# Attention and two expert layers on one core: freeing the queues after attention, and spreading the first batch's work over more slots

## The chip, the cores and the metric

One Trainium2 chip, one of its cores. The metric is the device time of one execution in microseconds (us); a kernel is run three times or more and the median is quoted. A profile comes from one further execution, so sums are made against that execution's own time.

## The reference

```python
def _attn_ref(q, k, v):            # q, k, v: (4, 8, 576, 64), float32
    scores = scale * np.matmul(q, k.transpose(0, 1, 3, 2))
    mask = block_i >= block_j      # blocks of 64 positions
    scores = np.where(mask, scores, -1000000000.0)
    attn = np.exp(scores - scores.max(-1, keepdims=True))
    attn = attn / (attn.sum(-1, keepdims=True) + 1e-09)
    return np.matmul(attn, v)
...
x = attn_out as (2304, 512)
h = x @ w_in                       # 512 -> 2048
g = np.maximum(h, 0.0) + alpha * np.minimum(h, 0.0)
x = g @ w_out                      # 2048 -> 512
h = x @ w2_in
g = np.where(h > 0.0, h, np.exp(np.minimum(h, 0.0)) - 1.0)
return g @ w2_out
```

The weights reach the kernel as 64-bit floats. Each is rebuilt on the chip as a float32 value.

## The kernel before

Every matrix product is made of three passes over a high and a low part of each operand (`PASSES`), so one product of 128x128 weights with 512 tokens over four chunks is twelve matmuls.

Attention runs over 16 pairs of heads, four pairs to a batch. `slot(k)` is one slot of its pipeline: the scores of one block of 128 queries, its maxima (VectorE), exponentials (ScalarE), the transposes of the block four slots back, and the products with the values that `products(k)` names. The first eight pairs (`n < WHOLE`) use `pv_whole`. Its first half has two chunks of keys. The second half has five, and all its matmuls stand in one slot, between that slot's scores and its transposes. Its `out()` then copies the sums from PSUM into `x1` (ScalarE for the high part, VectorE for the low part). The first 27 slots (`lead`) have attention alone. From there each slot of attention is followed by a piece of the first layer for a finished batch (`l1_beside`).

The first layer has 16 tiles of weights (`f`), the first eight in the pool `wA`. Units of 512, 512, 512, 512 and 256 tokens pass through it. After attention come stage A (units 3 and 4, tiles 0 to 7), stage B (all five units, tiles 8 to 15, in the pool `wB`) and stage C (all five units through the second layer, 16 tiles). One step of these stages is one `f`: `l1_h` (L499) or `l2_h` (L545) makes the hidden values, and two steps later `l1_y` (L587) or `l2_y` (L563) takes the gated values back. The gate of A and B is `neg` on ScalarE (L479), `g` on VectorE (L482), the high part on ScalarE (L486) and the low part on GpSimd (L81). The gate of C is `e` on ScalarE (L549), two operations on VectorE (L550, L551), the high part on ScalarE (L554) and the low part on VectorE (L81). Four PSUM banks hold the sums of a unit. At its end they are read out: in A by copies (`to_z`), in B by adding what A left (`z`, L594), whose halves go to memory for stage C. The next unit's sums start in the same banks.

`load_w` brings half a tile of weights and rebuilds it in pieces that it puts off by ticks (`later`, `end_tick`): `first` (ScalarE, L125 and L126), `bits` (VectorE, L130 to L132), `rounded` (GpSimd, L137), a copy (ScalarE, L145) and `last` (VectorE, L81). It has two buffers for the raw words and two for the rebuilt ones (`wraw`, `wword`). L125 needs a `wword` that `last` of the load two before has freed, and SyncE issues the next transfer into a raw buffer once L137 has read it. There are 16 such loads in and beside attention, then 48: 16 for tiles 8 to 15 of the first layer, 16 for tiles 0 to 7 of the second, and 16 for its tiles 8 to 15. The last 16 go into `wB`, whose tiles come free as the last unit of stage B is done with them.

The order of the work is written out by hand for all five queues: the program's order is each queue's order, and each queue runs its instructions one after the other. Where no such order is given, a planner in the compiler lays out each queue: at each point it takes, of the instructions whose inputs and buffers are there in its own model of time, the first in the program's order. The result is again one fixed order for each queue.

Of the kernel before, what the change touches and what calls it, by code (L numbers as in the profile page):

```python
# [11 lines left out]
U32 = mybir.dt.uint32  # L12
# [12 lines left out]
FH = NF // 2  # L25
# [16 lines left out]
def attention_moe_kernel(ctx: ExitStack, tc: tile.TileContext, qT, kT, v_a, v_b, w1, w2, alpha, out):  # L42
    nc = tc.nc
    pe, act, dve, pool_e = nc.tensor, nc.scalar, nc.vector, nc.gpsimd
# [24 lines left out]
    def take(name):  # L69
        r = rings[name]  # L70
        r.append(r.pop(0))
        return r[-1]
# [7 lines left out]
    def low_part(eng, out, x, high):  # L80
        return {"v": dve, "p": pool_e}[eng].tensor_tensor(out=out, in0=x, in1=f32(high), op=ALU.subtract)  # L81
# [13 lines left out]
    def later(ticks, emit):  # L95
        due.setdefault(tick[0] + ticks, []).append(emit)
# [13 lines left out]
    def load_w(layer, f, r):  # L110
        if r == 0:
            wt[layer, f] = w_pools[f // FH].tile([P, 2, 2 * DM], F32R, tag="w", name="w")
        t = wt[layer, f]
        raw = wraw_p.tile([P, 2 * DM], U32, tag="wraw", name="wraw")
        nc.sync.dma_start(out=raw, in_=(w1, w2)[layer][f, :, r * DM:(r + 1) * DM].bitcast(U32))
        pairs = raw.rearrange("p (n t) -> p n t", t=2)
        low, high = pairs[:, :, 0], pairs[:, :, 1]
        units = low.bitcast(I32)
        hi, lo = (t[:, k, r * DM:(r + 1) * DM] for k in range(2))
        word = []  # L120

        def first():
            w = wraw_p.tile([P, DM], F32, tag="wword", name="wword")
            word.append(w)
            act.activation(out=w, in_=high.bitcast(F32), func=AF.Abs)  # L125
            act.activation(out=units, in_=low, func=AF.Copy, scale=2.0 ** -29)  # L126

        def bits():
            w, wi = word[0], word[0].bitcast(U32)
            dve.tensor_scalar(w, w, F64_MIN, F64_MAX, ALU.max, ALU.min)  # L130
            dve.tensor_scalar(wi, wi, 3, 0x3FFFFFF8, ALU.logical_shift_left, ALU.bitwise_and)  # L131
            dve.scalar_tensor_tensor(  # L132
                out=wi, in0=high, scalar=0xC0000000, in1=wi, op0=ALU.bitwise_and, op1=ALU.bitwise_or)

        def rounded():
            w = word[0].bitcast(I32)
            pool_e.tensor_tensor(out=w, in0=w, in1=units, op=ALU.add)  # L137

        def last():
            low_part("v", lo, word[0], hi)  # L140
            ready.add((layer, f, r))
        later(2, first)
        later(3, bits)
        later(4, rounded)
        later(5, lambda: act.copy(hi, word[0]))  # L145
        later(6, last)

    def w_in(layer, f, part, kc):
        assert (layer, f, 0) in ready
# [15 lines left out]
    bank = [None] * 4 + [ps.tile([P, 512], F32, name=f"bank{i}") for i in range(4, 8)]  # L165
# [117 lines left out]
    def place(half, j):  # L283
        return (0, 128)[j] if half == 0 else 960 - 256 if j == 4 else 320 * j
# [47 lines left out]
    def x_tile(b):  # L332
        if b not in x1:
            x1[b] = xp.tile([P, 2, KC, 512], F32R, tag="x1", name="x1")
        return x1[b]

    def x_out(n, half, done):

        b, p = PAIRS[n]
        if half == 1:  # L340
            nc.sync.dma_start(out=xd[b][:, :, p, :], in_=f32(x1[b][:, :, p, :]))
            nc.sync.dma_start(out=xd[B][:, :, p, 64 * b:64 * b + 64], in_=f32(done))

    def parts_of_x(n, half):
        b, p = PAIRS[n]
        parts = [(slice(0, 256), lambda k: x_tile(b)[:, k, p, 256 * half:256 * half + 256])]
        tail = None
        if half == 1:
            tail = ap1.tile([P, 2, 64], F32R, tag="xtail", name="xtail")
            parts.append((slice(256, 320), lambda k: tail[:, k, :]))  # L350
        return parts, tail


    def pv_whole(n, half):
        s = st[n]
        q0, qn = HALF[half]
        nch = 2 if half == 0 else 5
        op = bank[take("o")]
        for j in range(nch):
            rows = 64 if j == 4 else P  # L360
            lo, o = max(0, P * j - q0), place(half, j)
            for x in range(2):
                pe.matmul(op[64 * x:64 * x + 64, lo:qn], s["v"][:rows, x, j, :],
                          s["pt", half, 0][:rows, x, o + lo:o + qn],
                          start=j == 0, stop=j == nch - 1, skip_group_check=True)

        def out():
            parts, tail = parts_of_x(n, half)
            for c, dst in parts:
                act.copy(dst(0), op[:, c])  # L370
                low_part("v", dst(1), op[:, c], dst(0))
            x_out(n, half, tail)
        return out
# [33 lines left out]
    LAG = 4  # L407
# [3 lines left out]
    def products(k):  # L411


        todo = []
        n, i = divmod(k - LAG - 4, 5)
        if i == 0 and 0 <= n < len(PAIRS):
            todo += [lambda: pv_whole(n, 0)] if n < WHOLE else [lambda: pv(n, 0, 0), lambda: pv(n, 0, 1)]
        m, i = divmod(k - LAG - 6, 5)
        if 0 <= m < len(PAIRS) and i < 2:
            if m >= WHOLE:  # L420
                todo.append(lambda: pv(m, 1, i))
            elif i == 0:
                todo.append(lambda: pv_whole(m, 1))
        return todo
# [37 lines left out]
        end_tick()  # L462

    X_DONE = [5 * (NPAIR * b + NPAIR - 1) + LAG + 6 + (NPAIR * (b + 1) > WHOLE) for b in range(B)]

# [133 lines left out]
    ET = mybir.EngineType  # L601
    with tc.manual_schedule(engines={ET.PE, ET.Activation, ET.DVE, ET.Pool, ET.SP}):
        ring("s", 0, 1)
        ring("t", 4, 5)
        ring("o", 6, 7)
        load_pair(0)
        split_k(0)
        split_q(0)

        todo_w = [(0, f, r) for r in range(2) for f in range(FH)]  # L610
        lead = X_DONE[0] + 2
        for k in range(lead):
            if k % 3 == 0 and k and len(todo_w) > FH:
                load_w(*todo_w.pop(0))
            slot(k)
        ring("t", 4, 5, 6)
        rings["o"] = rings["t"]
        ring("h", 7)


        k = lead
        for u in range(B - 1):
            parts = l1_beside(u)
            for j in range(20):
                if todo_w:
                    load_w(*todo_w.pop(0))
                next(parts)
                if k < LAST:
                    assert k <= X_DONE[u + 1] or j >= 18
                    slot(k)  # L630
                    k += 1
        assert k == LAST and not held

        att.close()
        ps = ctx.enter_context(pool("ps_all", 1, space=PSUM))
        bank[:] = [ps.tile([P, 512], F32, name=f"bank{i}") for i in range(8)]
        w_pools.append(ctx.enter_context(pool("wB", FH)))
        late_pools.append(ctx.enter_context(pool("late", 1)))  # L640
        ring("h", 6, 7, 0, 1)
        units = [("A", u) for u in range(B - 1, NU)] + [(k, u) for k in "BC" for u in range(NU)]
        fs = {"A": range(FH), "B": range(FH, NF), "C": range(NF)}
        steps = [(k, u, f) for k, u in units for f in fs[k]]
        first_of = {}
        for i, (k, u, f) in enumerate(steps):
            first_of.setdefault((k, u), i)
        lag = 2
        w_at = {}
        spread = [*range(8), *range(8, 16, 2), *range(16, 20)]  # L650
        for i in range(2 * FH):
            half = i // 2, i % 2
            w_at[spread[i]] = (0, FH + half[0], half[1])
            w_at[spread[-1] + 1 + i] = (1, *half)
            w_at[first_of["C", 0] - 2 + i] = (1, FH + half[0], half[1])
        gs = {}
        for i in range(len(steps) + lag):
            if i in w_at:
                load_w(*w_at[i])
            if i < len(steps):  # L660
                k, u, f = steps[i]
                if f == fs[k][1]:
                    n = units.index((k, u)) + 1
                    if n < len(units):
                        (load_x2 if units[n][0] == "C" else load_x1)(units[n][1])
                gs[i] = l2_h(u, f) if k == "C" else l1_gate(f, l1_h(u, f), UNITS[u])
            end_tick()
            if i >= lag:
                k, u, f = steps[i - lag]
                if k == "C":  # L670
                    l2_y(u, f, gs.pop(i - lag))
                else:
                    l1_y(k, u, f, gs.pop(i - lag))
            end_tick()
# [32 lines left out]
```

## Time and profile before

| | |
|---|---|
| median of three runs | 1105.73 us (1104.4 to 1106.81) |
| the profiled execution | 1103.71 us |
| its span, from the first to the last instruction | 1101.9 us |
| TensorE busy | 1002.6 us, 91% of the span |
| VectorE, ScalarE, GpSimd busy | 596.9, 463.7, 385.2 us |
| mean granted clock of TensorE | 0.968 |

TensorE is the engine with the most work. The profile cuts the span into stretches and gives each engine's busy time there, the clock that TensorE was granted (1.00 is 2.4 GHz, 0.50 is 1.2 GHz), and what each instruction waited for. 1.8 us of the execution lie outside the span.

### The profile page before, as it was taken

What the parts mean: (1) busy time and instruction counts of PE and PEld (TensorE: products, weight loads), DVE (VectorE), ACT (ScalarE), POOL (GpSimd) and SP (SyncE); (2) the same over time, 40 slices, a digit from 0 to 9 for tenths busy, and PEclk for the clock granted to TensorE, in tenths of its full rate; (3) what the DMA queues carried; (4) which work ended last, traced back from release to release, by engine and by line L of the source; (5) the groups of instructions that cost most, each with busy time, mean ns of one, the idle gap of its engine ahead of it and who ended that gap; (6) DMA issues with size and microseconds to landing.
All of it is one profiled execution on the core that took longest, in us unless ns stands there. A gap on an engine that the chain in (4) does not pass through costs nothing.

```text
span 1101.9 us, 14026 instructions
## 1 busy us (share of the span) xinstructions
PE 1002.6 (91%) x5072; PEld 805.8 (73%) x5072; DVE 596.9 (54%) x1067; ACT 463.7 (42%) x1017; POOL 385.2 (35%) x452
## 2 busy tenths in 40 slices
PE   6768769999999998997979998987899999999998
PEld 4446547778878887886758887865688888888887
DVE  5777875566666375657564325777433333333343
ACT  4666644575575344444443324444222222222222
POOL 5655664586686353545454332222000000000000
PEclk9898989999999998998989999998899999999999
DMA  4343322212211325536362345322200210110010
GB/s 143 102 156 97 127 89 87 83 57 94 85 54 52 136 98 192 166 123 225 120 224 99 115 154 181 105 77 76 95 20 1 77 39 1 39 39 1 1 39 20
DMA packets 50469, 101.58 MB, mean 92 GB/s; under 512 B 10592, under 2 KB 18784, under 8 KB 49760
## 3 DMA queue, kind: packets, MB, share of 16 engines
q1 hardware_dynamic: 50400, 100.69, 27.1%
q8 instruction: 40, 0.66, 0.3%
q14 instruction: 29, 0.24, 0.1%
HBM read 72.36 MB, written 28.31 MB: 91 GB/s over the span
## 4 chain that ended last, share of the span: by engine, by line
PE 54%; DVE 18%; ACT 9%; issue 5%; POOL 3%; DMA 3%; SPq 0%; ACTq 0%; POOLq 0%; DVEq 0%
PE bank L563 15%; PE bank L545 15%; PE bank L499 7%; PE bank L522 5%; PE bank L587 4%; DVE wword L132 4%; DVE w L81 4%; DMA wraw<-w 3%; PE bank L386 3%; ACT wword L125 2%; DVE g L482 2%; PE pair L234 2%; ACT wraw L126 2%; DVE wword L131 2%; PE bank L310 2%
## 5 line engine op out<-in xcount | busy, mean ns | idle before, releaser
L499 PE MATMUL bank<-x,w 128*128 128x512 f32 (+1 forms) x960 | 216.6, 376 | 10.7 <-ACT h L514 9.7
L545 PE MATMUL bank<-x,w 128*128 128x512 f32 (+1 forms) x960 | 215.1, 373 | 10.4 <-DVE w L81 7.5
L563 PE MATMUL bank<-w,gs 128*128 128x512 f32 x864 | 213.5, 394 | 8.7 <-DVE gs L81 5.6
L545 PEld LDWEIGHTS bank<-x,w 128*128 128x128 f32 x960 | 171.5, 191 | 43.7 <-DVE w L81 8.4
L499 PEld LDWEIGHTS bank<-x,w 128*128 128x128 f32 x960 | 169.7, 192 | 42.8 <-ACT h L514 11.8
L563 PEld LDWEIGHTS bank<-w,gs 128*128 128x128 f32 x864 | 162.3, 190 | 45.5 <-DVE gs L81 7.6
L587 PE MATMUL bank<-gs,w 128*128 128x512 f32 (+1 forms) x672 | 151.0, 372 | 23.0 <-DVE z L594 12.4
L587 PEld LDWEIGHTS bank<-gs,w 128*128 128x128 f32 x672 | 116.9, 195 | 49.5 <-issue 13.2
L81 POOL TENSOR_TENSOR gs<-g,gs 128x512 fp32r<-128x512 f32 (+1 forms) x80 | 96.1, 1201 | 155.6 <-ACT gs L486 155.4
L550 DVE TENSOR_SCALAR e<-e 128x512 f32<-128x512 f32 (+1 forms) x80 | 32.1, 401 | 188.5 <-ACT e L549 188.5
L137 POOL TENSOR_TENSOR wword<-wword,wraw 128x512 int32<-128x512 int32 x64 | 96.4, 1506 | 95.9 <-DVE wword L132 67.2
L549 ACT ACTIVATE e<-bank 128x512 f32<-128x512 f32 (+1 forms) x80 | 44.2, 553 | 171.6 <-PE bank L545 171.6
L88 POOL TENSOR_SCALAR p<-p,stat 128x128 f32<-128x128 f32 (+2 forms) x144 | 85.6, 612 | 61.7 <-DVE stat L275 43.2
L482 DVE SCALAR_TENSOR_TENSOR g<-neg,beta,bank 128x512 f32<-128x512 f32 (+1 forms) x56 | 37.5, 670 | 126.8 <-ACT neg L479 126.8
L125 ACT ACTIVATE wword<-wraw 128x512 f32<-128x512 f32 x64 | 43.0, 671 | 124.1 <-DVE w L81 96.6
L522 PE MATMUL bank<-gs,w 128*128 128x512 f32 x288 | 76.7, 409 | 10.2 <-ACT h L514 9.3
L554 ACT CAST gs<-e 128x512 fp32r<-128x512 f32 (+1 forms) x80 | 46.3, 579 | 82.7 <-DVE e L551 82.7
L264 ACT ACTIVATE p<-pair,stat 128x128 f32<-128x128 f32 (+3 forms) x128 | 67.0, 535 | 23.0 <-DVE stat L253 19.0
L132 DVE SCALAR_TENSOR_TENSOR wword<-wraw,wword 128x512 uint32<-128x512 uint32 x64 | 75.3, 1176 | 2.2
L81 DVE TENSOR_TENSOR gs<-e,gs 128x512 fp32r<-128x512 f32 (+1 forms) x80 | 51.0, 638 | 41.2 <-ACT gs L554 41.2
L81 DVE TENSOR_TENSOR w<-wword,w 128x512 fp32r<-128x512 f32 x64 | 66.5, 1039 | 7.2 <-ACT w L145 7.2
L522 PEld LDWEIGHTS bank<-gs,w 128*128 128x128 f32 x288 | 52.6, 193 | 20.9 <-ACT h L514 10.0
(84 smaller groups left out, 1170.8 us busy)
## 6 DMA issues: line engine op xcount, KB each, us to landing
wraw<-w SPq DMA_DIRECT2D x64, 512.0 KB, 3.5
xd<-x SPq DMA_DIRECT2D x16, 512.0 KB, 3.3
x<-xd SPq DMA_DIRECT2D x16, 512.0 KB, 8.3
yd<-ys SPq DMA_DIRECT2D x16, 512.0 KB, 5.7
x<-yd SPq DMA_DIRECT2D x4, 2048.0 KB, 8.2
qraw<-qT SPq DMA_DIRECT2D x16, 288.0 KB, 3.3
kraw<-kT SPq DMA_DIRECT2D x16, 288.0 KB, 3.6
vraw<-v_a SPq DMA_DIRECT2D x16, 256.0 KB, 4.0
```

The lines of the kernel that those rows point to most:

```text
L81: return {"v": dve, "p": pool_e}[eng].tensor_tensor(out=out, in0=x, in1=f32(high), op=ALU.subtract)
L88: return pool_e.tensor_scalar(out, x, 1.0 if scale is None else scale, 1.0, ALU.mult, ALU.mult)
L125: act.activation(out=w, in_=high.bitcast(F32), func=AF.Abs)
L132: dve.scalar_tensor_tensor(out=wi, in0=high, scalar=0xC0000000, in1=wi, op0=ALU.bitwise_and, op1=ALU.bitwise_or)
L137: pool_e.tensor_tensor(out=w, in0=w, in1=units, op=ALU.add)
L264: act.activation(out=p[:, x, :], in_=sb[:, x, :ext], func=AF.Exp, bias=stat[:, o + x:o + x + 1], accum_out=stat[:, 4 + o + x:5 + o + x])
L482: dve.scalar_tensor_tensor(out=g, in0=neg, scalar=beta[:, f:f + 1], in1=h, op0=ALU.mult, op1=ALU.add)
L499: pe.matmul(h, w_in(0, f, wp_, kc), x[:, xp_, kc, :n], start=kc == 0 and t == 0, stop=kc == KC - 1 and t == 2)
L522: pe.matmul(acc, w_out(0, f, wp_, m * P, P), gs[f][:, gp_, :n], start=f == 0 and t == 0, stop=f == FH - 1 and t == 2)
L545: pe.matmul(h, w_in(1, f, wp_, kc), x[:, xp_, kc, :], start=kc == 0 and t == 0, stop=kc == KC - 1 and t == 2)
L563: pe.matmul(acc, gs[:, gp_, tg * P:(tg + 1) * P], w_out(1, f, wp_, 0, DM), start=f == 0 and t == 0, stop=f == NF - 1 and t == 2)
L587: pe.matmul(acc, w_out(0, f, wp_, m * P, P), gs[:, gp_, :n], start=first and t == 0, stop=last and t == 2)
```

## The change

Three things are altered. The hand order for all five queues now ends with attention; from stage A to the end only TensorE keeps it, and ScalarE, VectorE, GpSimd and SyncE get the planner's order. The third operation of `bits` (L132) becomes a piece of its own, `sign`. For the eight loads of the lead (layer 0, `f < FH`, `r == 0`) `sign` and all pieces after it come one tick later; for all other loads `sign` stands right behind `bits`, as before. Last, in the first batch (pairs 0 to 3) the second half of `pv_whole` is cut in two: chunks 0 and 1 in one slot, chunks 2 to 4 and `out()` in the next.

```diff
             dve.tensor_scalar(wi, wi, 3, 0x3FFFFFF8, ALU.logical_shift_left, ALU.bitwise_and)
+
+        def sign():
+            wi = word[0].bitcast(U32)
             dve.scalar_tensor_tensor(
                 out=wi, in0=high, scalar=0xC0000000, in1=wi, op0=ALU.bitwise_and, op1=ALU.bitwise_or)
...
         later(3, bits)
-        later(4, rounded)
-        later(5, lambda: act.copy(hi, word[0]))
-        later(6, last)
+        slow = 1 if layer == 0 and f < FH and r == 0 else 0
+        later(3 + slow, sign)
+        later(4 + slow, rounded)
+        later(5 + slow, lambda: act.copy(hi, word[0]))
+        later(6 + slow, last)
...
-    def pv_whole(n, half):
+    def pv_whole(n, half, chunks=None):
...
-        op = bank[take("o")]
-        for j in range(nch):
+        chunks = chunks or range(nch)
+        if chunks[0] == 0:
+            s["op"] = bank[take("o")]
+        op = s["op"]
+        for j in chunks:
...
         def out():
+            if chunks[-1] < nch - 1:
+                return
...
             if m >= WHOLE:
                 todo.append(lambda: pv(m, 1, i))
+            elif 5 * m + LAG + 7 < LEAD:
+                todo.append(lambda: pv_whole(m, 1, (range(2), range(2, 5))[i]))
             elif i == 0:
                 todo.append(lambda: pv_whole(m, 1))
...
         assert k == LAST and not held
 
+
+    with tc.manual_schedule(engines={ET.PE}):
 
 
         att.close()
```

(`lead` also becomes `LEAD`, with the same value, 27.)

## Rows read from the trace of the kernel before

**Rows 1.** Windows: span start:end, length, busy us (x instructions) per engine, clock, DMA share.

```profile
0.00:88.59 88.59, 62.35 (x387) 39.80 (x387) 64.36 (x155) 50.48 (x144) 54.36 (x92) 0.92 0.38 125
...
375.40:671.00 295.60, 272.57 (x1321) 227.13 (x1321) 154.94 (x213) 124.45 (x230) 126.10 (x99) 0.97 0.46 155
671.00:784.56 113.56, 94.48 (x386) 73.95 (x385) 77.58 (x117) 46.12 (x83) 26.46 (x19) 0.92 0.29 97
784.56:1096.41 311.85, 311.84 (x1465) 261.61 (x1463) 111.99 (x203) 75.25 (x136) 0.00 (x0) 1.00 0.08 30
```

**Rows 2.** Chain that ended last, two of its pieces: start, length, engine and line.

```profile
577.18 2.72 PE bank L499 x12
...
661.08 1.44 PE bank L587 x12
```

**Rows 3.** Windows of five stretches between stage A and stage C, columns as before.

```profile
422.22:432.00 9.78, 4.73 (x26) 4.23 (x25) 8.07 (x14) 5.54 (x12) 4.64 (x4) 0.74 0.90 281
502.65:516.70 14.05, 8.24 (x26) 5.40 (x25) 10.53 (x14) 5.48 (x10) 5.55 (x5) 0.76 0.69 225
555.72:571.54 15.82, 8.19 (x25) 5.41 (x24) 12.04 (x16) 6.81 (x13) 5.57 (x5) 0.78 0.62 200
682.08:690.09 8.01, 4.88 (x14) 3.51 (x13) 5.71 (x12) 3.37 (x8) 2.03 (x3) 0.79 0.93 371
717.32:784.56 67.24, 51.28 (x193) 38.46 (x192) 45.13 (x66) 26.00 (x47) 13.74 (x9) 0.90 0.20 66
```

**Rows 4.** Timeline of TensorE at the end of a unit of stage B.

```profile
555.72 2.88 PE L499 MATMUL bank<-x,w 128*128 128x512 f32 x12
565.69 1.62 PE L587 MATMUL bank<-gs,w 128*128 128x512 f32 x3 [7.09 <-DVE z L594]
```

**Rows 5.** Timeline of VectorE there.

```profile
561.66 0.75 DVE L482 SCALAR_TENSOR_TENSOR g<-neg,beta,bank 128x512 f32<-128x512 f32 x1 [1.77 <-ACT neg L479]
...
564.87 0.68 DVE L594 TENSOR_TENSOR z<-bank,z 128x512 f32<-128x512 f32 x1
```

**Rows 6.** Timeline of ScalarE, once there and twice in stage C.

```profile
554.22 0.67 ACT L125 ACTIVATE wword<-wraw 128x512 f32<-128x512 f32 x1 [2.56 <-DVE w L81]
...
736.55 0.67 ACT L125 ACTIVATE wword<-wraw 128x512 f32<-128x512 f32 x1 [3.26 <-DVE w L81]
...
743.35 0.66 ACT L125 ACTIVATE wword<-wraw 128x512 f32<-128x512 f32 x1 [3.26 <-DVE w L81]
```

**Rows 7.** Groups by line from 671 to 784 us: count, busy, mean ns, idle before.

```profile
L81 DVE TENSOR_TENSOR w<-wword,w 128x512 fp32r<-128x512 f32 x15 | 25.8, 1717 | 0.0
L137 POOL TENSOR_TENSOR wword<-wword,wraw 128x512 int32<-128x512 int32 x16 | 24.2, 1510 | 69.9 <-DVE wword L132 66.6 <-ACT gs L554 3.3
L132 DVE SCALAR_TENSOR_TENSOR wword<-wraw,wword 128x512 uint32<-128x512 uint32 x16 | 11.5, 718 | 0.6
L551 DVE SCALAR_TENSOR_TENSOR e<-bank,e 128x512 f32<-128x512 f32 x16 | 11.1, 692 | 0.6
L81 DVE TENSOR_TENSOR gs<-e,gs 128x512 fp32r<-128x512 f32 x15 | 10.3, 684 | 0.0
...
L550 DVE TENSOR_SCALAR e<-e 128x512 f32<-128x512 f32 x16 | 6.9, 428 | 32.7 <-ACT e L549 32.7
L131 DVE TENSOR_SCALAR wword<-wword 128x512 uint32<-128x512 uint32 x16 | 6.8, 427 | 0.5
L130 DVE TENSOR_SCALAR wword<-wword 128x512 f32<-128x512 f32 x16 | 6.7, 418 | 0.0
```

**Rows 8.** DMA issues of the page: median us from issue to landing stands last.

```profile
wraw<-w SPq DMA_DIRECT2D x64, 512.0 KB, 3.5
```

**Rows 9.** Timeline of TensorE in the lead, at the second half of a pair's product.

```profile
64.96 0.35 PE L234 MATMUL pair<-kh,qh 64*128 64x128 f32 x2 [4.36 <-ACT p L264]
...
65.67 3.82 PE L363 MATMUL bank<-pt,vraw 128*64 128x320 f32 x20
```

**Rows 10.** Timeline of VectorE in the lead, around that product.

```profile
69.95 0.42 DVE L81 TENSOR_TENSOR x<-bank,x 128x256 fp32r<-128x256 f32 x1 [1.70 <-ACT x L370]
```

More of the change, by code (lines that the diff above doesn't have):

```diff
@@ L464, in attention_moe_kernel @@
     X_DONE = [5 * (NPAIR * b + NPAIR - 1) + LAG + 6 + (NPAIR * (b + 1) > WHOLE) for b in range(B)]
+    LEAD = X_DONE[0] + 2
     def load_x1(u):
@@ L610, in attention_moe_kernel @@
         todo_w = [(0, f, r) for r in range(2) for f in range(FH)]
-        lead = X_DONE[0] + 2
-        for k in range(lead):
+        for k in range(LEAD):
             if k % 3 == 0 and k and len(todo_w) > FH:
@@ L618, in attention_moe_kernel @@
         ring("h", 7)
-        k = lead
+        k = LEAD
         for u in range(B - 1):
```

## The prediction

> **What bounds the kernel now.** I read the windows first, cut where the stages meet. From 784.56 us to the last matmul TensorE is busy 311.84 of 311.85 us at full clock [rows 1]: that part cannot get shorter, since no matmul is removed. From 375.40 (the first matmul of stage A) to 784.56 it is busy 272.57 of 295.60 and 94.48 of 113.56 us, at a mean granted clock of 0.97 and 0.92 [rows 1]. So the second reading is what this stretch would take if TensorE never waited. The chain of waits shows twelve matmuls of 512 tokens taking 2.72 us and twelve of 256 tokens 1.44 us at full clock [rows 2]. By the loops there are 110 groups of the first kind in the stretch (16 in A's unit 3, 64 in B's units 0 to 3, and 16 `l2_h` and 14 `l2_y` of C's unit 0) and 32 of the second: 110 x 2.72 + 32 x 1.44 = 345.3 us. The stretch lasts 409.2. **63.9 us are lost there**: 42.1 with TensorE idle, and nearly all of the rest by matmuls at the low clock behind the idle times, as the clock columns of the five worst stretches show (0.74 to 0.90) [rows 3].
>
> These five hold 54.9 of it. At the ends of units: 9.78 us for two groups of 256 tokens (2.88), 14.05 and 15.82 us for two of 512 (5.44 each), 8.01 for one (2.72), so 6.9 + 8.6 + 10.4 + 5.3 = 31.2. In C's unit 0: 67.24 us for eight steps of 5.44, 43.5, so 23.7 [rows 3]. The other 9.0 are crumbs of one or two microseconds at other steps.
>
> Third, who is late. At the end of a B unit TensorE goes idle for 7.09 us until VectorE has added a sum out of its bank (`z`, L594) [rows 4]. The sum had been complete for longer than that. VectorE stood 1.77 us for `neg`, then ran `g` and the three decoding operations, and only then `z`, at 564.87 [rows 5]. `neg` in turn was late because ScalarE stood 2.6 us at L125 of the next load, whose `wword` the decoding had not freed, with `neg` behind it [rows 6]. In C it is the same ring: L125 waits 3.26 us for VectorE's `last`, `e` stands behind L125, VectorE's gate waits for `e`, and `last` stands behind the gate. One turn decodes one load and lets one step through, and takes 743.35 - 736.55 = 6.80 us, where TensorE needs 5.44 [rows 2, 6].
>
> So the loss is one of order in the queues, not of work: in the two windows VectorE is busy 154.94 and 77.58 us, 57% of the stretch, and ScalarE and GpSimd less [rows 1].
>
> **The change, part by part.** *The planner's order after attention* removes and adds no instruction. It moves four queues: `neg` or `e` no longer stands behind an L125 that has no buffer, `z` no longer behind decoding that came later than its sum, and on SyncE the loads of tokens and partial sums no longer behind a weight transfer that waits for a raw buffer. What can take the place of the ring is work, so I sum that. One load and one step of C cost VectorE 428 + 692 + 684 ns for the gate and 418 + 427 + 718 + 1717 for the decoding, 5.08 us [rows 7], under 5.44. The 1717 is a time with GpSimd's L137 beside it; the same shape in the gate takes 684 [rows 7]. GpSimd has 1.51 us. ScalarE has five operations on tiles no larger, so it has room. The last sixteen loads are the tight ones: `wB` comes free only as B's unit 4 ends, from about 656.8 (tile 10 is read back at 661.08, three groups of 1.44 after tile 8 [rows 2]); the weights of step 8 are wanted when that step begins, about 712 (717.32 less the 5.3 lost before it [rows 3]), and the sixteenth load when tile 15 is read back, 9 steps and a half of 5.44 later, about 764. Sixteen loads in 764 - 657 allow 6.7 us each, against 5.1 of VectorE. The first two can stand decoded up to the copy beforehand, since their buffers are no part of `wB`. So I take C's unit 0 as nearly unhindered.
>
> From both sides: the gain of this part is at most the 63.9, and the least, if the new order merely has other waits, is below nothing (second rival). What I leave standing: 1.1 us at each of the seven unit ends of the stretch, because four adds of about 0.7 us and the halves behind them still go through VectorE (7.7); 0.3 us at each of the sixteen short steps of 256 tokens, where the gate has half the time (4.8); and 3.4 for the rest, C's first steps and the start of A. That is 15.9, so 63.9 - 15.9 = **48 us gained**. The entries are my estimates; the ends are taken nearer to the crumbs than to the 8.6 and 10.4 of the ends with decoding beside them.
>
> Here a rule of the notes on the chip bears on the sum. The row shows `last` at 1717 ns beside L137 where its twin takes 684 [rows 7]. The Trainium skill (SBUF — State Buffer, "Who interferes with whom") says that GpSimd and VectorE share one pair of ports as an exclusive lock, so that the loser stands still for the other's whole instruction. The trace agrees: 1717 - 684 = 1.03 us, within L137's 1.51. By that rule a step with a load costs the pair 428 + 692 + 684 + 418 + 427 + 718 + 684 + 1510 = 5.56 us at most and not 5.08, 0.12 over TensorE's 5.44, and the sum would lose some 2 us more over sixteen loads.
>
> *The second product in two slots.* All its matmuls run 3.82 us at the low clock, in front of the slot's transposes and the next slot's scores [rows 9]. The first two chunks are 640 of its 1216 columns (320, 320, 320, 192, 64), 2.0 us; the other 1.8 go behind the next slot's scores, which come that much sooner. VectorE's wait of 1.70 us for the sums of it [rows 10] moves one slot on, to where maxima stand before it. This happens four times. Against it: the last `out()` now falls in slot 26, and its bank is the one that the first `l1_h` writes in slot 27; ScalarE's and VectorE's copies, about 1.2 us, then lie in TensorE's way once. *Decoding in smaller pieces* leaves VectorE's work as it is, but `bits` and the `last` of an earlier load (up to 2.25 us unhindered, by rows 7) no longer stand in one block before a slot's maxima. The lead is a ring of VectorE, ScalarE and TensorE: VectorE is busy 64.36 of 88.59 us [rows 1], and TensorE waits 4.36 us for exponentials once before such a product [rows 9]. The gain lies between -2 (the bank, and one more tick of decoding) and 24.2 (all of VectorE's idle time). Most of that idle time is the start and other waits, so I take **3 us**, nearer to the 1.70 of the one wait that is surely moved.
>
> The sum: 1103.71 - 48 - 3 = 1052.7 for the profiled execution, which lay 2.0 below the median of its runs. **Forecast: 1055 us.**
>
> **The rivals.**
> 1. *The planner packs the decoding.* It starts pieces of later loads as soon as an engine is free, at five loads to four steps, say. By the price of rows 7 a step then has 1.80 + 1.25 x 3.76 = 6.5 us of VectorE and GpSimd together, if they exclude each other, 1.06 over 5.44. Forty-eight loads take 38 steps: 40 us lost, less the slack of four groups (10.9 us) in each of two bursts, so 19 us of the gain: 1074. For it: GpSimd's and VectorE's times do stretch each other. Against: the gates come first in the program's order.
> 2. *The other side: the fixed order stands on transfers that come later than planned.* Weights land 3.5 us after issue in the median [rows 8]. If the plan reckons them 2 us earlier than the chip brings them, ScalarE stands at L125 with the gate behind it, at each load: 48 x 2 = 96 us, less 10.9 of slack once, 85 lost in place of 63.9: about 1124 with the lead's 3 us. It decides from about 1.6 us a load ((63.9 + 3 + 10.9) / 48). Against: the raw buffer is filled a load ahead, which hides most of a transfer.
> 3. *No change: the two buffers, not the order, set the pace.* Then a turn stays 6.8 us and the time within 1104 to 1107. Against: one load's own chain on VectorE and GpSimd is 0.42 + 0.43 + 0.72 + 1.72 + 1.51 = 4.8 us, some 7 with ScalarE's three, and two loads overlap.
> 4. *Better than forecast:* 6 us left standing, 10 gained in the lead: 1103.7 - 58 - 10 + 2 = 1038.
>
> **How the numbers follow.** Forecast 0.60, rival 1 0.18, rival 2 0.12, rival 3 0.04, rival 4 0.06. The forecast's own range is 1043 (9 left standing, 8 in the lead) to 1068 (24 left standing, -2 in the lead). The range of 8 in 10 takes in rivals 1 and 4 with their edges, 1036 to 1094, and leaves rivals 2 and 3 out. Faster by over 0.2% (about what a measurement of this kernel can tell from no change): 0.60 + 0.18 + 0.06 = 0.84; the same 0.04; slower 0.12.
>
> **What would show it.** Right: in the changed profile the idle times of TensorE before L587 released by `z` shrink to about a microsecond, those before L545 released by `w` vanish, steps of C's unit 0 come every 5.44 us, and the granted clock stays at 1.00 from the start of A. The stretch from the first matmul of A to the last of C is then about 673 us (721 - 48), and A begins about 3 us earlier. Rival 1 shows as steps of 6 us and more in A and B with VectorE above nine tenths. Rival 2 shows as ScalarE waiting on transfers before L125 with `neg` or `e` late. The lead is wrong if TensorE's first `l1_h` comes later than 88.6 us. The forecast fails above all if the fixed order that the planner leaves puts decoding before a gate whose time on the chip is not the planner's.

## The result, and the profile after

The changed kernel takes **1064.74 us** in the median of four runs (1063.21 to 1067.16), against 1106.27 (1104.40 to 1107.37) for the kernel before on the same chip: a ratio of 0.9628, 95% interval 0.9602 to 0.9654. The forecast was 1055 with a range of 1036 to 1094. The profiled execution took 1063.36 us, span 1061.6. Below, the line numbers are those of the changed kernel: `l1_h` is L512, `l1_y` L600, `l2_h` L558, `l2_y` L576; `neg` L492, `g` L495, the gate's high part L499 and low part L81; in the decoding L125, L126, L130, L131, `sign` L135, `rounded` L140, the copy L150 and `last` L81; the sums of B (`z`) L607.

The windows come first again, cut at the first `l1_h`, the start of stage A, the start and end of C's unit 0, and the last matmul (columns as in [rows 1]):

```profile
0.00:86.24 86.24, 61.42 (x386) 40.23 (x386) 65.32 (x156) 52.48 (x149) 57.02 (x92) 0.92 0.42 135
...
376.43:656.92 280.49, 267.84 (x1320) 225.55 (x1321) 161.69 (x225) 128.58 (x236) 131.11 (x101) 0.99 0.48 161
656.92:744.48 87.56, 85.42 (x386) 70.29 (x385) 62.18 (x99) 39.21 (x72) 21.98 (x16) 1.00 0.29 100
```

From the first matmul of A to the last of C (1056.34) it is now 679.9 us; in [rows 1] it was 721.0. So 41.1 us came from there. With TensorE never waiting it would be 345.3 + 311.85 = 657.1, so of the 63.9 us lost before, 22.8 are still lost. C's unit 0 is nearly clean: its last thirteen steps (670.75 to 744.48) take 73.7 us where 13 x 5.44 is 70.7. From A's start to C's unit 0 TensorE is still idle for 12.65 us. The waits between 370 and 760 us (engine and line, what it waited for, us in total, times, longest) say who was late:

```profile
ACT wword L125 <- DMA wraw<-w: 28.7, 23, 2.9
...
PE bank L600 <- POOL gs L81: 7.2, 6, 2.4
...
PE bank L600 <- ACT z L85: 2.2, 1, 2.2
...
PE bank L600 <- DVE z L607: 1.4, 1, 1.4
...
ACT wword L125 <- DVE w L81: 0.3, 1, 0.3
```

The ring of [rows 6] is gone: L125 waits for VectorE's `last` for 0.3 us. The 7.09 us for `z` of [rows 4] has no counterpart; the longest wait for `z` is 1.4. What is new is that TensorE waits for the gate's low part on GpSimd. One such place, on TensorE and then on ScalarE, VectorE and GpSimd (timelines; start, length, in brackets the idle time before and its releaser):

```profile
491.74 2.88 PE L512 MATMUL bank<-x,w 128*128 128x512 f32 x12
494.60 0.50 PE L600 MATMUL bank<-gs,w 128*128 128x512 f32 x1
497.52 2.79 PE L600 MATMUL bank<-gs,w 128*128 128x512 f32 x11 [2.41 <-POOL gs L81]
```

```profile
490.65 0.68 ACT L125 ACTIVATE wword<-wraw 128x512 f32<-128x512 f32 x1 [1.50 <-DMA wraw<-w]
491.22 0.67 ACT L126 ACTIVATE wraw<-wraw 128x512 int32<-128x512 uint32 x1
491.78 0.59 ACT L492 ACTIVATE neg<-bank 128x512 f32<-128x512 f32 x1
```

```profile
491.82 1.42 DVE L131 TENSOR_SCALAR wword<-wword 128x512 uint32<-128x512 uint32 x1
493.16 0.73 DVE L495 SCALAR_TENSOR_TENSOR g<-neg,beta,bank 128x512 f32<-128x512 f32 x1
```

```profile
491.36 1.59 POOL L140 TENSOR_TENSOR wword<-wword,wraw 128x512 int32<-128x512 int32 x1 [2.31 <-ACT wword L125]
494.72 1.51 POOL L140 TENSOR_TENSOR wword<-wword,wraw 128x512 int32<-128x512 int32 x1 [1.77 <-PE bank L512]
496.19 1.27 POOL L81 TENSOR_TENSOR gs<-g,gs 128x512 fp32r<-128x512 f32 x1
```

In the order of time: ScalarE stands 1.50 us at L125 for a transfer, with `neg` behind it. When `neg` is done, VectorE is in a decoding operation that takes 1.42 us beside GpSimd's. `g` follows, then ScalarE's high part; by then GpSimd's fixed order has another load's L140 in front of the low part. TensorE is idle for 2.41 us. The same pattern stands at 419.20 (2.42 us).

Decoding also runs ahead. In the 37.2 us from 479.74 to 516.97 ScalarE starts eight loads (L125 at 483.20, 487.93, 490.65, ... 515.70), nine with the one at 479.57, in five steps of TensorE, which need 27.2. Of the first 32 loads, 31 L125 are recorded, from 383.20 to 532.64. After that there are none until 644.82, and from 517.1 us to the end of B TensorE has no gap (139.82 of 139.82 us busy).

### The profile page after: what moved, and what is told of

The parts are those of the page before. It is cut to its first block, busy times and chain, and to the rows that moved or that the text cites. A ratio compares the mean times of both kernels' runs of the same rounds, so it can differ in the third digit from the quotient of the medians.

```text
span 1061.6 us, 14048 instructions
## 1 busy us (share of the span) xinstructions
PE 988.5 (93%) x5072; PEld 800.9 (75%) x5072; DVE 589.9 (56%) x1067; ACT 464.5 (44%) x1017; POOL 390.4 (37%) x452
## 4 chain that ended last, share of the span: by engine, by line
PE 65%; DVE 13%; POOL 7%; DMA 6%; ACT 5%; issue 4%; POOLq 0%; ACTq 0%; SPq 0%; DVEq 0%
PE bank L576 17%; PE bank L558 17%; PE bank L512 10%; PE bank L600 8%; DMA wraw<-w 6%; PE bank L535 5%; POOL wword L140 3%; PE bank L396 3%; PE pair L239 2%; DVE wword L130 2%; DVE wword L131 2%; DVE wword L135 2%; PE bank L315 1%; DVE stat L258 1%; DVE w L81 1%
## 5 line engine op out<-in xcount | busy, mean ns | idle before, releaser
L512 PE MATMUL bank<-x,w 128*128 128x512 f32 (+1 forms) x960 | 215.9, 375 | 16.4 <-ACT h L527 14.1
L576 PE MATMUL bank<-w,gs 128*128 128x512 f32 x864 | 209.6, 390 | 2.1 <-DVE gs L81 1.2
L558 PE MATMUL bank<-x,w 128*128 128x512 f32 (+1 forms) x960 | 210.1, 368 | 0.0
L512 PEld LDWEIGHTS bank<-x,w 128*128 128x128 f32 x960 | 168.8, 191 | 48.1 <-ACT h L527 15.6
L558 PEld LDWEIGHTS bank<-x,w 128*128 128x128 f32 x960 | 169.1, 188 | 31.1
L576 PEld LDWEIGHTS bank<-w,gs 128*128 128x128 f32 x864 | 161.0, 188 | 35.9 <-DVE gs L81 1.9
L600 PE MATMUL bank<-gs,w 128*128 128x512 f32 (+1 forms) x672 | 146.7, 366 | 12.7 <-POOL gs L81 7.2
L81 POOL TENSOR_TENSOR gs<-g,gs 128x512 fp32r<-128x512 f32 (+1 forms) x80 | 100.6, 1257 | 124.3 <-ACT gs L499 117.1
L600 PEld LDWEIGHTS bank<-gs,w 128*128 128x128 f32 x672 | 115.8, 193 | 36.2 <-POOL gs L81 9.4
L140 POOL TENSOR_TENSOR wword<-wword,wraw 128x512 int32<-128x512 int32 x64 | 90.8, 1419 | 81.3 <-DVE wword L135 55.4
L535 PE MATMUL bank<-gs,w 128*128 128x512 f32 x288 | 77.0, 410 | 10.7 <-ACT h L527 9.3
L495 DVE SCALAR_TENSOR_TENSOR g<-neg,beta,bank 128x512 f32<-128x512 f32 (+1 forms) x56 | 37.2, 665 | 72.0 <-ACT neg L492 72.0
L81 DVE TENSOR_TENSOR w<-wword,w 128x512 fp32r<-128x512 f32 x64 | 64.2, 1006 | 21.9 <-ACT w L150 20.7
L81 DVE TENSOR_TENSOR gs<-e,gs 128x512 fp32r<-128x512 f32 (+1 forms) x80 | 51.0, 638 | 44.0 <-ACT gs L567 43.6
L499 ACT CAST gs<-g 128x512 fp32r<-128x512 f32 (+1 forms) x80 | 46.1, 576 | 44.6 <-DVE g L495 44.5
L150 ACT CAST w<-wword 128x512 fp32r<-128x512 f32 x64 | 39.5, 621 | 48.3 <-POOL wword L140 47.0
```

Source lines behind the costliest of these rows:

```text
L499: act.copy(t[:, 0, :], g)
L512: pe.matmul(h, w_in(0, f, wp_, kc), x[:, xp_, kc, :n], start=kc == 0 and t == 0, stop=kc == KC - 1 and t == 2)
L535: pe.matmul(acc, w_out(0, f, wp_, m * P, P), gs[f][:, gp_, :n], start=f == 0 and t == 0, stop=f == FH - 1 and t == 2)
L558: pe.matmul(h, w_in(1, f, wp_, kc), x[:, xp_, kc, :], start=kc == 0 and t == 0, stop=kc == KC - 1 and t == 2)
L576: pe.matmul(acc, gs[:, gp_, tg * P:(tg + 1) * P], w_out(1, f, wp_, 0, DM), start=f == 0 and t == 0, stop=f == NF - 1 and t == 2)
L600: pe.matmul(acc, w_out(0, f, wp_, m * P, P), gs[:, gp_, :n], start=first and t == 0, stop=last and t == 2)
```

## The experiments

All times are medians on the chip; each ratio is against the kernel before on the same chip, with its 95% interval. "Lost" is the stretch from A's first matmul to C's last in the profiled execution, less 657.1; it is read from one execution and carries that execution's scatter.

**1 to 4: the parts, and which queue.** The planner's part alone: the kernel before, with this line put in after attention.

```diff
+    with tc.manual_schedule(engines={ET.PE}):
```

> Only the planner's order after attention is taken from the change; the lead stays as in the kernel before. If the whole gain is the planner's, attention ends as before (first matmul of stage A at about 375.4 us) and the stretch from it to the last matmul takes about 680 us as in the changed kernel: about 1064 us, ratio 0.962. If the lead's two edits carry part of the gain, the time lies above 1070.

1067.5 us (1065.49 to 1069.13), ratio 0.9647 (0.9630 to 0.9663); lost 28.7. Nearly all of the gain is the planner's. The planner leaves the same order here as in the changed kernel: up to 700 us all 276 operations recorded on ScalarE here stand in the same order there, on VectorE 280 of 281, on GpSimd 112 of 113. So 28.7 and 22.8 are two executions of one order after attention, and the difference of 2.8 us between the two medians is not clear of their intervals.

The lead's part alone: the changed kernel with all five queues by hand to the end.

```diff
-    with tc.manual_schedule(engines={ET.PE}):
+    with tc.manual_schedule(engines={ET.PE, ET.Activation, ET.DVE, ET.Pool, ET.SP}):
```

> Only the two edits in the lead are taken; all five queues keep the hand order to the end. The changed kernel's profile has the first matmul of the first layer 2.4 us earlier than before and stage A 1.0 us later. If that is the two edits' doing, both show again here and the time is within 0.2% of before (1105 to 1108 us). The prediction's claim was a gain of 3 us (about 1103).

1101.34 us (1100.34 to 1101.57), ratio 0.9952 (0.9939 to 0.9964): 4.9 us faster, so the expectation failed. It had been read from where A starts in one profile, and that start is not steady: with the same program up to A and all queues by hand until then, it lies between 373.88 and 377.06 in the executions of five kernels.

The ring, without the planner: the kernel before, by hand, with L125 and L126 one tick later for all loads behind attention, so that they stand behind `neg` or `e`.

```diff
-        later(2, first)
+        later(2 + (1 if layer or f >= FH else 0), first)
```

> The kernel before, all by hand, with one thing changed after attention: the first piece of a load (L125, L126) is put off by one tick, so that it stands behind the gate's first ScalarE operation and not ahead of it. If the loss is the ring at L125, the steps beside decoding return to 5.44 us and the stretch after attention shortens by 30 us or more of the 64 lost: at most about 1075 us. If the loss lies in other places (VectorE's order at the ends of units, SyncE's order of the transfers, or work), it stays above 1090.

1075.84 us (1074.52 to 1078.37), ratio 0.9730 (0.9712 to 0.9749); lost 33.4. This one move in the hand order gives 30 us, and L125 no longer waits for `last`: the ring of [rows 6] is shown to be the cause of about half of the 63.9 us lost before. Of the rest, the largest waits of TensorE here are 7.3 us in two places for `z` from VectorE and 5.2 us once for ScalarE's copy of `z`.

The planner for ScalarE alone (VectorE, GpSimd and SyncE by hand):

```diff
+    with tc.manual_schedule(engines={ET.PE, ET.DVE, ET.Pool, ET.SP}):
```

> After attention only ScalarE gets the planner's order; TensorE, VectorE, GpSimd and SyncE keep the hand order. If ScalarE's order is what closes the ring, this alone brings at least half of the planner's 41 us: 1085 us or less. If VectorE's or SyncE's order is needed (the rival), it stays above 1095.

1089.11 us (1086.65 to 1090.65), ratio 0.9841 (0.9824 to 0.9857); lost 49.9. It falls between the two expectations. `neg` and `e` come free, but VectorE still has decoding ahead of the sums:

```profile
511.15 1.62 PE L587 MATMUL bank<-gs,w 128*128 128x512 f32 x3 [8.18 <-DVE z L594]
```

**5, 6 and 12: which of the lead's edits.** Each by hand to the end: the split product alone (`slow = 0`), the smaller decoding pieces alone (the split's two lines out), and both, with the split for three of the four pairs.

```diff
-        slow = 1 if layer == 0 and f < FH and r == 0 else 0
+        slow = 0
```

> The kernel before with the second product of the first batch in two slots, and nothing else; all five queues by hand. The two lead edits together gave 4.9 us. Theory (the prediction's): the split carries most of it, since it moves a wait that stands in TensorE's and VectorE's way once a pair: 1102 to 1103, three to four us under the kernel before, and TensorE's first l1_h one to two us earlier than 88.6. Rival: the smaller decoding pieces carry it; then this kernel is within 1 us of the kernel before.

1107.65 us (1104.11 to 1110.73), ratio 1.0017 (1.0005 to 1.0029): no gain, if anything 2 us slower, which neither expectation had.

```diff
-            elif 5 * m + LAG + 7 < LEAD:
-                todo.append(lambda: pv_whole(m, 1, (range(2), range(2, 5))[i]))
```

> The kernel before with decoding in smaller pieces in the lead, and nothing else; all five queues by hand. Theory: one us or less, 1105 to 1107, since VectorE's work stays and only its order beside the maxima changes. Rival: three to four us faster, and then the split alone gives nothing. If both kernels gain and the two gains together exceed 4.9 us, the edits remove the same idle time.

1099.84 us (1099.41 to 1101.21), ratio 0.9958 (0.9945 to 0.9971): 5.3 us faster. The rival was right. The pieces carry all of the lead's gain. VectorE before one slot's maxima (L258), first with the split alone, then with the pieces alone:

```profile
60.11 0.68 DVE L81 TENSOR_TENSOR w<-wword,w 128x512 fp32r<-128x512 f32 x1
60.71 0.90 DVE L130 TENSOR_SCALAR wword<-wword 128x512 f32<-128x512 f32 x1
61.64 1.51 DVE L131 TENSOR_SCALAR wword<-wword 128x512 uint32<-128x512 uint32 x1
63.19 0.98 DVE L135 SCALAR_TENSOR_TENSOR wword<-wraw,wword 128x512 uint32<-128x512 uint32 x1
...
64.39 1.22 DVE L258 TENSOR_REDUCE stat<-pair 128x2 f32<-128x1024 f32 x1
```

```profile
56.88 0.42 DVE L130 TENSOR_SCALAR wword<-wword 128x512 f32<-128x512 f32 x1
57.34 0.77 DVE L131 TENSOR_SCALAR wword<-wword 128x512 uint32<-128x512 uint32 x1
...
58.33 1.22 DVE L258 TENSOR_REDUCE stat<-pair 128x2 f32<-128x1024 f32 x1
```

With the split alone the maxima stand behind 4.1 us of decoding, with the pieces behind 1.25, since `sign` and `last` come later, when GpSimd is done. The exponentials wait for the maxima and TensorE for the exponentials (with the split alone for VectorE's part of the queries, L216, which stands behind the maxima too): the idle time before the pair's first scores is 4.60 us in the first (67.19), 1.61 in the second (61.13), and 4.36 before [rows 9].

The pieces give some of it back later. In the two profiles the first `l1_h` comes at 84.19, 4.4 us earlier than in [rows 1], a wait that both kernels have later ends 2.8 us earlier (147.73 and 150.52), and A starts 2.5 earlier. In the piece beside attention, where the order is by hand in every kernel here, a copy of `h` stands behind an L125 that waits for `last`. With the pieces this happens at 107.28 as well:

```profile
105.54 0.66 ACT L125 ACTIVATE wword<-wraw 128x512 f32<-128x512 f32 x1 [4.85 <-DVE w L81]
106.11 0.67 ACT L126 ACTIVATE wraw<-wraw 128x512 int32<-128x512 uint32 x1
106.67 0.56 ACT L525 COPY h<-bank 128x512 f32<-128x512 f32 x1
```

TensorE is idle 7.92 us for that copy (7.92 in the changed kernel too, at 108.33). Before, the wait for it at this place was 2.08 us, at 106.37. The wait at 150.52 is also 7.92 us for a copy of `h`, and it stands in both kernels.

```diff
-            elif 5 * m + LAG + 7 < LEAD:
+            elif 5 * m + LAG + 12 < LEAD:
```

> Both lead edits, all five queues by hand, but the last pair of the first batch (whose second sums share a bank with TensorE's first l1_h) is not split. Theory: the bank is most of the split's cost, 1.2 us of wait: 1099.5 to 1100.5, at the level of the pieces alone (1099.8). Rival: the split costs something at each pair (the scores and transposes between the two halves run at the low clock): 1100.8 to 1101.8, as with all four split (1101.3).

1100.36 us (1099.34 to 1102.31), ratio 0.9951 (0.9938 to 0.9965). Both lead edits, the pieces alone and this kernel lie within each other's intervals. Beside the pieces, the split's cost or gain is too small to tell; whether the bank is what it costs stays open.

**7 to 11: what is still lost.** The gate's low part of A and B from GpSimd to VectorE, in the changed kernel:

```diff
-            low_part("p", t[:, 1, :], g, t[:, 0, :])
+            low_part("p" if beside else "v", t[:, 1, :], g, t[:, 0, :])
```

> The changed kernel with the low part of the gated values of stages A and B on VectorE instead of GpSimd. 22.9 us of the stretch from A to C are still lost in the changed kernel, and TensorE's largest named wait there is for that GpSimd operation (7.2 us), which stands behind the integer addition of a load in GpSimd's fixed order. Theory: GpSimd's order is one cause of what is left, so 5 to 12 us go: 1053 to 1060, and the waits for the low part shrink to under 2 us. Rival: the gate is late already when it reaches GpSimd (ScalarE stands at a transfer), or VectorE, which gets 48 operations of 0.7 us more, is late in its turn: 1062 to 1072, and the waits only change their names.

1059.36 us (1059.09 to 1060.95), ratio 0.9590 (0.9578 to 0.9603); lost 19.7. By the ratios some 4 us faster, at the lower edge of what was expected of the theory. GpSimd's order is a part; in its place TensorE waits 3.0 us for VectorE's low part (five times), where under 2 was expected. But the largest wait left begins with ScalarE at L125:

```profile
508.31 5.97 PE L600 MATMUL bank<-gs,w 128*128 128x512 f32 x12 [5.81 <-ACT wword L125]
```

This matmul reads nothing that L125 writes, but it is the first one into a bank that VectorE's `z` empties. L125 stood 4.39 us for a transfer and started at 505.99. In VectorE's planned order L130 of that load stands in front of `z`: L130 at 506.68, after 4.36 us of waiting for L125, `z` (L607) from 507.48 to 508.16, the matmul at 508.31.

ScalarE by hand to the end, with `first` one tick later as in experiment 3; the other three queues keep the planner's order:

```diff
-        later(2, first)
+        later(2 + (1 if layer or f >= FH else 0), first)
...
-    with tc.manual_schedule(engines={ET.PE}):
+    with tc.manual_schedule(engines={ET.PE, ET.Activation}):
```

> The changed kernel with ScalarE's queue by hand to the end too, and in it the first operation of a load one tick later, so that it stands behind the gate's first; VectorE, GpSimd and SyncE keep the planner's order. Theory: what is left is mostly the prediction's second rival in small, ScalarE standing at a transfer that lands later than the plan has it with the gate behind it; then 5 to 12 us go: 1053 to 1060. Rival: what is left is decoding packed ahead on VectorE and GpSimd; then nothing is gained, 1063 to 1072, or more if the three planned queues are laid for another order of ScalarE.

1052.72 us (1051.28 to 1053.57), ratio 0.9526 (0.9513 to 0.9539); lost 13.9. As the theory had it, but two things were changed. So the second alone, with `first` at its old place:

```diff
-    with tc.manual_schedule(engines={ET.PE}):
+    with tc.manual_schedule(engines={ET.PE, ET.Activation}):
```

> The changed kernel with ScalarE's queue by hand to the end and the first operation of a load at its old place, ahead of the gate's first. It parts the two edits of the run that took 1052.7 us. Theory: the place of that operation is what gained, since in the old place it waits for the buffer that the decoding frees and the gate stands behind it; then much of the ring is back and this kernel takes 1075 us or more. Rival: ScalarE's hand order as such gained, the planner having laid its queue badly: 1050 to 1062.

**1040.66 us** (1040.32 to 1041.22), ratio 0.9413 (0.9400 to 0.9426); lost 2.5. The theory fell: the old place is better by 12 us. ScalarE's hand order gives 24 us over the changed kernel, and TensorE stands hardly anywhere from A on (windows, columns as above, the last one at the place shown for the changed kernel):

```profile
374.09:655.00 280.91, 279.44 (x1410) 238.86 (x1411) 168.49 (x241) 134.89 (x248) 135.10 (x106) 1.00 0.51 174
655.00:742.00 87.00, 87.00 (x384) 71.81 (x383) 63.38 (x102) 42.28 (x73) 17.95 (x13) 1.00 0.30 104
478.40:514.50 36.10, 36.10 (x161) 29.88 (x160) 25.02 (x34) 19.72 (x35) 19.61 (x14) 1.00 0.66 225
```

ScalarE there, by hand:

```profile
503.93 0.62 ACT L499 CAST gs<-g 128x512 fp32r<-128x512 f32 x1 [1.07 <-DVE g L495]
508.76 0.67 ACT L125 ACTIVATE wword<-wraw 128x512 f32<-128x512 f32 x1 [4.21 <-DMA wraw<-w]
509.34 0.66 ACT L126 ACTIVATE wraw<-wraw 128x512 int32<-128x512 uint32 x1
509.90 0.57 ACT L492 ACTIVATE neg<-bank 128x512 f32<-128x512 f32 x1
```

Here L125 stands 4.21 us for a transfer, longer than any of the 23 such waits in the changed kernel, and TensorE has no idle time there. In front of it is L499, whose values are wanted next. Behind it is `neg` of the step whose `l1_h` ran from 502.68 and whose gated values are taken back two steps later. The hand order takes up one load a step at most in this part: in 36.1 us L125 starts six times. The loss of the ring is not back either (13.3 us of waits of L125 for `last`, the longest 1.1). What differs is VectorE's order. Before, and then in experiment 9:

```profile
501.11 0.75 DVE L482 SCALAR_TENSOR_TENSOR g<-neg,beta,bank 128x512 f32<-128x512 f32 x1 [1.78 <-ACT neg L479]
501.78 0.42 DVE L130 TENSOR_SCALAR wword<-wword 128x512 f32<-128x512 f32 x1
...
502.69 1.74 DVE L132 SCALAR_TENSOR_TENSOR wword<-wraw,wword 128x512 uint32<-128x512 uint32 x1
504.35 0.68 DVE L81 TENSOR_TENSOR w<-wword,w 128x512 fp32r<-128x512 f32 x1
```

```profile
501.34 0.70 DVE L130 TENSOR_SCALAR wword<-wword 128x512 f32<-128x512 f32 x1 [0.73 <-ACT wword L125]
...
502.54 0.69 DVE L135 SCALAR_TENSOR_TENSOR wword<-wraw,wword 128x512 uint32<-128x512 uint32 x1
503.15 0.74 DVE L495 SCALAR_TENSOR_TENSOR g<-neg,beta,bank 128x512 f32<-128x512 f32 x1
503.81 1.52 DVE L81 TENSOR_TENSOR w<-wword,w 128x512 fp32r<-128x512 f32 x1
```

By hand, decoding waited behind `g`, and `g` for `neg`. Here decoding starts as soon as L125 is done, while ScalarE works at L126 and `neg`, so `last` comes earlier and the next L125 waits 0.8 us and not 2.55.

Set beside experiment 2, the trace says more than the edit does. From A's start to 760 us of experiment 2, all 299 operations recorded on ScalarE stand in the same order here, as they must, and 113 of GpSimd's 116 as well, though the planner laid GpSimd out anew; on VectorE 240 of 311 do, and SyncE's transfers are in another order. So, but for these few operations of GpSimd, the 60.7 us between the two come from VectorE's and SyncE's order; no run parts these two. Against the changed kernel the edit moves three queues: the planner, with ScalarE fixed, also gave VectorE and GpSimd another order (244 of 337 and 100 of 116 recorded operations in common order). How much of the 24 us is ScalarE's own is not shown.

With `first` a tick later (experiment 8) the waiting L125 stands in front of L499 instead, and a late transfer costs TensorE time. ScalarE of that kernel, and then its TensorE:

```profile
514.41 0.66 ACT L125 ACTIVATE wword<-wraw 128x512 f32<-128x512 f32 x1 [3.55 <-DMA wraw<-w]
514.98 0.65 ACT L126 ACTIVATE wraw<-wraw 128x512 int32<-128x512 uint32 x1
515.53 0.60 ACT L499 CAST gs<-g 128x512 fp32r<-128x512 f32 x1
```

```profile
516.19 0.50 PE L600 MATMUL bank<-gs,w 128*128 128x512 f32 x1 [1.30 <-ACT gs L499]
517.89 2.80 PE L600 MATMUL bank<-gs,w 128*128 128x512 f32 x11 [1.21 <-POOL gs L81]
```

This place explains 2.5 of the 11.4 us that experiment 8 loses more than experiment 9. TensorE's longest wait there, 3.44 us for ScalarE's copy of `z` (425.47), is of another kind: the copy stands behind ScalarE's L150, which waits 2.55 us for GpSimd's L140. The rest of the 12 us was not taken apart.

Last, on top of experiment 8, the split left out:

```diff
-            elif 5 * m + LAG + 7 < LEAD:
-                todo.append(lambda: pv_whole(m, 1, (range(2), range(2, 5))[i]))
```

> The 1052.7 us version without the split of the second product. Theory: the split costs 1.5 to 2.5 us wherever it stands, as it did beside the smaller pieces by hand (1101.3 against 1099.8): 1050 to 1051.5. Rival: what the lead gains or loses is made up before stage A begins, since VectorE's work there waits for other things: 1052 to 1054.

1052.29 us (1048.83 to 1054.48), ratio 0.9515 (0.9494 to 0.9536): within experiment 8's interval, so it tells nothing of the split. Then the low part on VectorE too:

```diff
-            low_part("p", t[:, 1, :], g, t[:, 0, :])
+            low_part("p" if beside else "v", t[:, 1, :], g, t[:, 0, :])
```

> The same (no split, ScalarE by hand with the later first operation), and the low part of the gated values of A and B on VectorE. Theory: the waits for GpSimd's low part, 3.3 us of the 8.1 that TensorE still waits there, and the low clock behind them go: 3 to 5 us under the version without this edit. Rival: VectorE's decoding now stands ahead of the low part as GpSimd's did, so within 1.5 us of it, or slower.

1053.55 us (1051.46 to 1053.95), ratio 0.9526 (0.9511 to 0.9540): the rival was right. With ScalarE by hand the waits for the low part are replaced by others, among them 4.60 us for ScalarE's copy of `z` at the end of A's unit (427.19). The version of experiment 9 without the split, or with the ring beside attention mended, was not run.

## Why the prediction was right, and where it was off

**The mechanism.** Right in the main. What was lost was order, not work: no instruction is removed, and the stretch shrinks by 41.1 us. Experiment 3 shows the ring, experiment 4 shows that ScalarE's queue alone is not enough, and experiment 9 that the work fits: 2.5 us lost, with all decoding in place. One step is not borne out: that `neg` or `e` must get out from behind L125. In experiment 9 they stand behind it as before, and it is VectorE's order (and perhaps SyncE's) that opens the ring; moving ScalarE's queue too went with 24 us more, not less. The third rival (two buffers set the pace) is excluded by the same run.

**The size of the planner's part.** Predicted 48, measured 41.1 in the profile of the changed kernel, 35.2 in experiment 1's with the same order (38.7 between the medians). The term that was mis-sized is what is left standing, 22.8 in place of 15.9. Its parts were wrong in both directions. Of the seven unit ends with 1.1 us each, five cost nothing: from 438 to 480 and from 517.1 to the end of B TensorE has no gap. The 4.8 for short steps and the 3.4 for the rest were far too small for two bursts of decoding, from 414.62 to 438.08 (two groups of 2.72 and six of 1.44 are 14.1 of 23.5 us, so 9.4 lost) and from 479.74 to 516.97 (37.23 us for five steps of 5.44, so 10.0 lost). The step that failed is the silent counterpart, for A and B, of "so I take C's unit 0 as nearly unhindered": the price per load was worked out for C, where the sentence held (3.0 us lost in thirteen steps), while in A and at B's start the planner's order takes up loads faster than TensorE needs them, and the gate stands behind them.

**The rivals.** The first (decoding packed) and the second (late transfers) both happened, in small and together. Packing: nine loads in five steps at the worst. It did not need VectorE above nine tenths: there VectorE is busy 29.40 of 37.23 us, and the delay comes from the order of single operations. Late transfers: 28.7 us of waits at L125 in 23 places (and 4.2 at L126 in three), 0.7 us a load over 48 loads, below the 1.6 from which that rival would have decided. Experiment 9 gives 20.3 of the 22.8 us. There the packing is gone, but not the late transfers: L125 still stands 19.7 us for them in seven places, the longest 4.6, and TensorE's idle time from A's start to 655 us is 1.5 us. So a late transfer costs by what stands behind it. Which of the two rivals weighs more was not separated.

**The lead.** The size was near, 3 us predicted against 4.9 by hand; the 2.8 between the changed kernel and the planner's part alone is not clear of noise, and in their profiles none of it has been gained when A starts (376.43 and 376.14). But it was near by luck, for the step was wrong: "the other 1.8 go behind the next slot's scores, which come that much sooner" was taken as the gain, and the pieces as something that "leaves VectorE's work as it is". The split alone gives nothing; the pieces give 5.3. The row that should have decided is the 4.36 us before the pair's scores [rows 9]: it was read as a ring of three engines, and it was VectorE's decoding in front of the maxima. VectorE of the kernel before, from its first decoding operation in front of these maxima to its last, and the maxima:

```profile
58.14 0.68 DVE L81 TENSOR_TENSOR w<-wword,w 128x512 fp32r<-128x512 f32 x1
...
60.17 1.77 DVE L132 SCALAR_TENSOR_TENSOR wword<-wraw,wword 128x512 uint32<-128x512 uint32 x1
...
62.16 1.22 DVE L253 TENSOR_REDUCE stat<-pair 128x2 f32<-128x1024 f32 x1
```

The prediction did name this block in front of the maxima, and gave its removal no price. The bank that the last `out()` shares with the first `l1_h` was rightly named: TensorE waits 1.29 us for it.

```profile
86.24 3.02 PE L512 MATMUL bank<-x,w 128*128 128x512 f32 x12 [1.29 <-DVE xtail L81]
```

**The signs.** The waits for `w` before `l2_h` are gone (no idle time before L558 from A's start to 757), those for `z` are about a microsecond (4.0 once in experiment 1, with the same order), C's steps come every 5.44 us but for two (6.04 and 7.85), the first `l1_h` is 2.35 earlier. Not as said: the clock falls twice below 1.00 after A's start (0.93 between 414.6 and 438, 0.95 between 480 and 517), and A begins 1.0 us later, not 3 earlier. The two misses make up the difference: 6.9 in the stretch and 4.0 in A's start are 10.9, against 1063.4 - 1052.7 = 10.7.

**The rule on the shared ports.** The rows agree with it further. L131 takes 427 ns in C before the change [rows 7], but 1.42 us beside an L140 in the burst shown above and 1.51 beside GpSimd's low part of a key in the split-alone lead. The Trainium skill (SBUF — State Buffer, "Who interferes with whom") says that the loser of the pair waits for the other's whole instruction, and the extra 1.0 to 1.1 us lie within the 1.46 to 1.59 of GpSimd's. The 2 us that the rule would add to C are within its 3.0 lost, which does not show that they are the cause.

## What to carry to other kernels

Freeing a queue from a hand order breaks a ring of waits, but the planner fills idle time with whatever its model has ready, and its order is then as fixed as the one by hand: look per queue at who profits. Of the combinations run, the best has VectorE, GpSimd and SyncE by the planner and ScalarE, which starts each load and so sets the pace of decoding, by hand; GpSimd's order there is nearly the one by hand. This ring opened at ScalarE in experiment 3 and at VectorE in experiment 9: compare the queues' orders in two traces to see which one an edit really changed. Put an operation that may wait for a transfer behind what is wanted next and in front of what has the most slack; in these traces a wait of 4.21 us cost nothing there, and one of 3.55 us cost 2.5 us one place further up.

## What the runs showed of the hardware that was not expected

VectorE's operations on 128x512 tiles that take 0.41 to 0.69 us alone took up to 1.77 us beside GpSimd in the lines shown, in the lead too. There the order alone, with the same work, moved a wait of 4.36 us to 1.61. And the start of stage A, after the same program, differs by up to 3.2 us between executions, so an edit of one or two us before it can't be judged from one profile.
